# Mixture-of-experts after windowed attention: an earlier second routing phase, four weight fetches on the first queue, and a small gather ahead

## The chip, the core and the metric

The kernel runs on one core of one Trainium2 chip. The metric is the device time of one execution in microseconds; the time before is 681.13 us, the median of three runs. A core has a matmul engine (PE), two elementwise engines (VectorE, DVE here, and ScalarE, ACT here), GpSimd (POOL), and SyncE (SP), which issues DMAs. Each engine takes its instructions in program order; an instruction that waits for another engine holds everything queued behind it on its own engine.

## The reference

Attention over a window of 64 keys gives 4608 rows of 512 values. A gate of 512x8 scores every row for eight experts. The (row, expert) pairs are taken in the order of falling score: a row goes to the expert if it has no expert yet and the expert has fewer than 576 rows. Each expert then runs a two-layer network on its rows.

```python
logits = x @ w_gate
order = np.argsort(-logits.flatten())
for idx in order:
    tok, e = (int(idx) // E, int(idx) % E)
    if assigned[tok] >= 0 or counts[e] >= cap:
        continue
    assigned[tok] = e
    counts[e] += 1
for e in range(E):
    mask = assigned == e
    h = np.maximum(x[mask] @ w1[e], 0.0)
    out[mask] = h @ w2[e]
```

## The kernel before

**Stages.** Attention (to about 160 us) leaves the rows in DRAM as `xs` and the scores in SBUF as `L`. Routing runs in eight phases p = 0 to 7; each finds the expert that fills up next, writes its number to `ei`, and lists its 576 rows in `idx`. Then that expert's rows are gathered, transposed and multiplied, while the routing of later phases goes on between the products. Phase 0 has nothing to run beside; from phase 1 on, routing instructions stand between matmuls of the experts.

**A routing phase** (`Routing.steps`). Phase 1 begins with six operations that find each row's best open expert (`choices`, L446 to L453). Then come eight rounds of a search for the threshold score. In phase 1 a round is: VectorE compares all scores with 15 thresholds (`G`, L461, two instructions), PE counts with nine small matmuls (L532, `rps`), VectorE folds the counts down to `pr` (L538 to L564), PE spreads the result over all partitions (L567), and VectorE picks the next thresholds (L572 to L590). After the rounds come positions (L643, L644), the list (L681, L690) and `idx` (L695). A phase's tail (L702 to L725, one matmul L720 in it) takes the filled expert out of `L`; the next phase needs that.

**An expert.** `turn` gathers the rows with five indirect DMAs issued by POOL (`xg`, L849), PE transposes each (L862, `tp`), ACT takes the high part of the transposed rows (`xh`, L839) and VectorE the rest (`xl`, L843). `load` fetches eight weight chunks of 512 KB into six stage buffers `st` (L780, from SP; for p = 0 from POOL from the fourth chunk on, behind the gathers on POOL). ACT makes each chunk's high part `wh` (L797). The low part `wl` is a VectorE subtraction for the first three chunks of the first expert (L801); for all others ACT writes the negated high part (L806) and POOL issues a DMA that adds the stage buffer to it (L808). `steps` runs 16 units of the first layer (L908: twelve matmuls each, as wh with xh, wl with xh, wh with xl; the unit waits in a PSUM buffer `h`, of which there are three, for ACT's `hh`, L880, and VectorE's `hl`, L885), then the second layer (L940 for the last 64 rows, L950 for the rest).

**What sets the order.** Nothing is scheduled on the chip. `Streams` runs the generators `route`, `load`, `turn` and `steps` against a modelled clock while the program is built: a generator that yields a number is resumed that many nanoseconds later, one that yields a function when it turns true. The order of these resumptions is the order of instructions on every engine. `slack` (from `SLACK[p]`, 0 for the first phase and 100 for the others) is added to the modelled time at several places of every round. Phase 1 is held by `yield lambda: ex.turned` in `route` until the first expert's rows are all transposed. The first expert's chunk 3 is held by the same condition in `load`, and its chunks 3 to 7 follow at 3500 modelled nanoseconds each.

Of the kernel before, what the change touches and what calls it, by code (L numbers as in the profile page):

```python
# [25 lines left out]
DM = H * D  # L26
# [314 lines left out]
NR = 8  # L341
FAR = 2.0 ** 101
OWN = 2
SLACK = (0,) + (100,) * 7
U32 = mybir.dt.uint32


class Routing:


    def __init__(self, ctx, tc, c, V):
        self.tc, self.nc, self.c, self.V = tc, tc.nc, c, V
        nc = tc.nc
        rt = ctx.enter_context(tc.tile_pool(name="rt", bufs=1))
        self.rt, self.ctx = rt, ctx

        def t(name, shape, dt=FT):
            x = rt.tile(shape, dt, name=name)
            setattr(self, name, x)
            return x  # L360

        for name in ("eid", "un", "m", "best"):
            t(name, [128, NJ])
        for name in ("oh", "w", "one"):
            t(name, [128, NJ, E], BF)
        t("G0", [128, NJ, ND], BF)
        t("cw", [128, E])
        t("dg", [128, ND], I32)
        t("lane", [128, 1])
        self.setup = self.constants(c["jp"], t)  # L370
        self.idx, self.eint = {}, {}

    def counters(self):
        iota = self.nc.gpsimd.iota
        iota(self.cw, pattern=[[-1, E]], base=E, channel_multiplier=0, allow_small_or_imprecise_dtypes=True)
        iota(self.dg, pattern=[[1, ND]], base=1, channel_multiplier=0)
        iota(self.lane, pattern=[[0, 1]], base=0, channel_multiplier=1, allow_small_or_imprecise_dtypes=True)

    def constants(self, jp, t):
# [103 lines left out]
    def steps(self, p):  # L483
# [7 lines left out]
        if p < E - 1:  # L491
# [6 lines left out]
            if own:  # L498
                one4 = tile_([128, NJ // 4, 4, 4 * E], BF, name="one4")
                one1 = one.rearrange("p (q k) e -> p q (k e)", k=4)  # L500
                for j0, j1 in ((0, 3), (3, 6), (6, 9)):
                    nc.scalar.copy(one4[:, j0:j1], one1[:, j0:j1, None, :].to_broadcast([128, 3, 4, 4 * E]))
                yield 2000
            M = 128 if own else 32
            q8 = self.all8
            thr = self.tab[:, 0]
            base = tile_([128, 1], I32, name="base")
            rest = []
            for r in range(NR):
                G = tile_([128, NJ, ND], BF, name="G") if p or r else self.G0  # L510

                if not p:
# [183 lines left out]
        self.idx[p] = idx  # L696
        yield self.dve(200)
        if p < E - 1:
            if p == 0:
                yield 3000  # L700
            if not p:
                nc.vector.scalar_tensor_tensor(self.eid, m, T[:, 0:1], best, op0=OP.is_gt, op1=OP.mult)  # L702
            eq = tile_([128, NJ], FT, name="eq")
# [31 lines left out]
NCH = 4  # L735
# [11 lines left out]
class Experts:  # L747
# [17 lines left out]
    def room(self):  # L765
        return self.ps.tile([128, 320], FT, name="h", bufs=3)

    def load(self, p, ei):

        nc, fw = self.nc, self.fw  # L770
# [5 lines left out]
        def fetch(i):  # L776
            st[i] = fw.tile([128, 1024], FT, name="st", bufs=STAGE)

            q, r = (nc.gpsimd, eg) if p == 0 and i >= 3 else (nc.sync, e)
            q.dma_start(st[i], self.part(i, r))  # L780

            there[i] = max(self.clock(), there.get(i - 1, 0)) + \
                (LOAD if p else 1500 if i < 3 else 4000) * (1 if i else 2)

        for i in range(3):
            fetch(i)
        if p == 0:
            yield lambda: self.gathered
        for i in range(2 * NCH):
            if p == 0 and i == 3:  # L790
                yield lambda: self.turned
            yield lambda: self.taken - self.ring < self.used
            if there[i] > self.clock():
                yield there[i] - self.clock()
# [14 lines left out]
                self.spawn(self.ready(p, i, hi, lo), self.busy(650, "pool") + ADDED - 1200)  # L809
                dt = 1300  # L810
            self.taken += 1
            if i + 3 < 2 * NCH:
                fetch(i + 3)
            yield max(100, dt - 1200) if p or i < 3 else 3500

    def ready(self, p, i, hi, lo):
        self.W[p, i] = (hi, lo)
# [175 lines left out]
def body(tc, q, k, v, vt, wg, w1, w2, xs, out):  # L993
    nc = tc.nc
    with ExitStack() as ctx:
# [12 lines left out]

        st = Streams()
        ex.spawn, ex.busy, rt.busy, ex.clock = st.add, st.busy, st.busy, lambda: st.now  # L1010
        ex.warm = rt.warm

        def route():
            for p in range(E):
                if p == 1:
                    yield lambda: ex.turned
                for dt in rt.steps(p):
                    if p in rt.eint and p not in known:
                        known.add(p)
# [32 lines left out]
```

## Time and profile before

| | us |
|---|---|
| median of 3 runs | 681.13 (680.34 to 681.78) |
| the profiled execution | 680.94 |
| its span, first to last instruction | 679.3 |
| PE busy in the span | 640.0 (94%) |
| VectorE, ScalarE, GpSimd busy | 444.7, 362.6, 184.2 |

The profiled execution's own time is 1.6 us over its span and 0.2 us under the median. A row of the timeline gives start, length, engine, line, operation, result and inputs, and in brackets the engine's idle time before it and what ended that. PE is busy 94% of the span, so what matters is where it is not, and where its granted clock is at the lower of its two levels (1.2 and 2.4 GHz; PEclk 1.00 is the upper one).

### The profile page before, as it was taken

The numbers are of one execution on the slowest core, as the hardware profiler recorded it, in microseconds if no ns is written. First come the engines' busy times: TensorE is split into PE (matmuls) and PEld (weight loads), VectorE is DVE, ScalarE is ACT, GpSimd is POOL, SyncE is SP. The second block draws the span as 40 slices with busy tenths as digits, with TensorE's granted clock in tenths as the row PEclk, the third lists the DMA queues.
The fourth block names the chain that finished last, engine by engine and source line by source line (L and its number), as shares of the span: only waits on it lengthen the run. The fifth ranks groups of instructions, "written<-read, shape, count | busy, mean of one in ns | idle before, by whom it ended". The sixth has DMA issues, their size and how long they took to land. (4 is left out here: it accounts for less than half of the span.)

```text
span 679.3 us, 16951 instructions
## 1 busy us (share of the span) xinstructions
PE 640.0 (94%) x6383; PEld 537.4 (79%) x6383; DVE 444.7 (65%) x2246; ACT 362.6 (53%) x733; POOL 184.2 (27%) x217
## 2 busy tenths in 40 slices
PE   7999999997489899799999999999999999999995
PEld 5667777775369678797898799789789879988984
DVE  5888898888767657586687688589668861220300
ACT  4788989884045328325743662753446455634410
POOL 0433133330042116204320630512233064312111
PEclk7999999998589999899999999999999999999999
DMA  9999998912066439907973983987696599972501
GB/s 299 346 368 370 368 325 318 350 65 80 16 235 136 90 120 276 240 2 254 239 145 110 261 199 69 299 196 140 229 226 148 159 247 288 239 203 77 95 24 46
DMA packets 50065, 134.08 MB, mean 197 GB/s; under 512 B 4672, under 2 KB 10944, under 8 KB 49984
## 3 DMA queue, kind: packets, MB, share of 16 engines
q0 software_dynamic: 15392, 53.49, 34.7%
q1 hardware_dynamic: 34048, 79.00, 33.0%
q8 instruction: 50, 0.82, 0.5%
q10 hardware_dynamic: 544, 0.52, 0.2%
q14 instruction: 31, 0.25, 0.1%
HBM read 82.13 MB, written 18.87 MB: 149 GB/s over the span
## 5 line engine op out<-in xcount | busy, mean ns | idle before, releaser
L930 POOL DMA_INDIRECT out<-ot,idx x40 | 41.2, 1029 | 262.1 <-DVE ot L928 48.1
L885 DVE SCALAR_TENSOR_TENSOR hl<-h,hh 128x256 fp32r<-128x256 f32 x128 | 53.4, 417 | 84.7 <-ACT hh L880 84.1
L880 ACT ACTIVATE hh<-h 128x256 fp32r<-128x256 f32 (+1 forms) x128 | 52.4, 409 | 101.5 <-PE h L908 100.2
L950 PE MATMUL o<-wh,hh 128*128 128x512 f32 x256 | 102.6, 401 | 0.0
L950 PE MATMUL o<-wh,hl 128*128 128x512 f32 x256 | 102.2, 399 | 0.0
L950 PE MATMUL o<-wl,hh 128*128 128x512 f32 x256 | 101.4, 396 | 0.0
L908 PE MATMUL h<-xh,wh 128*128 128x256 f32 (+1 forms) x512 | 92.9, 301 | 1.3 <-ACT xh L839 1.3
L135 DVE CUSTOM_DVE_ANT_0 st<-Sp,mask 128x128 f32<-128x128 f32 x288 | 78.7, 277 | 21.8 <-PE Sp L126 14.1
L908 PE MATMUL h<-xh,wl 128*128 128x256 f32 (+1 forms) x512 | 92.9, 300 | 0.0
L145 ACT ACTIVATE pe<-st,mx 128x128 f32<-128x128 f32 x288 | 91.2, 390 | 2.8 <-DVE mx L135 2.8
L908 PE MATMUL h<-xl,wh 128*128 128x256 f32 (+1 forms) x512 | 92.3, 299 | 0.1
L908 PEld LDWEIGHTS h<-xh,wh 128*128 128x128 f32 x512 | 76.1, 191 | 2.1 <-ACT xh L839 1.6
L908 PEld LDWEIGHTS h<-xh,wl 128*128 128x128 f32 x512 | 76.6, 191 | 0.1
L908 PEld LDWEIGHTS h<-xl,wh 128*128 128x128 f32 x512 | 76.2, 191 | 0.4 <-DVE xl L843 0.3
L797 ACT ACTIVATE wh<-st 128x1024 fp32r<-128x1024 f32 x64 | 67.2, 1051 | 10.7 <-DMA st<-w 10.6
L808 POOL DMA_DIRECT2D wl<-st x61 | 56.4, 1176 | 58.8 <-ACT wl L806 50.7
L922 ACT ACTIVATE ot<-o 128x512 f32<-128x512 f32 x32 | 19.1, 598 | 86.4 <-PE o L950 82.9
L806 ACT ACTIVATE wl<-wh 128x1024 fp32r<-128x1024 f32 x61 | 64.5, 1057 | 0.7
L849 POOL DMA_INDIRECT xg<-xs,idx x40 | 40.0, 1000 | 63.2 <-DMA st<-w 40.3
L950 PEld LDWEIGHTS o<-wh,hl 128*128 128x128 f32 x256 | 48.3, 189 | 9.8 <-issue 0.7
L950 PEld LDWEIGHTS o<-wh,hh 128*128 128x128 f32 x256 | 48.4, 189 | 8.8
L950 PEld LDWEIGHTS o<-wl,hh 128*128 128x128 f32 x256 | 48.3, 189 | 8.8
(175 smaller groups left out, 1135.7 us busy)
## 6 DMA issues: line engine op xcount, KB each, us to landing
wl<-st POOLq DMA_DIRECT2D x61, 512.0 KB, 8.1
st<-w SPq DMA_DIRECT2D x59, 512.0 KB, 7.7
xs<-x SPq DMA_DIRECT2D x36, 256.0 KB, 5.3
VO<-v SPq DMA_DIRECT2D x6, 1168.0 KB, 17.1
VT<-vt SPq DMA_DIRECT2D x6, 1152.0 KB, 11.7
Q<-q SPq DMA_DIRECT2D x6, 1152.0 KB, 14.1
K<-k SPq DMA_DIRECT2D x6, 1152.0 KB, 15.6
st<-w POOLq DMA_DIRECT2D x5, 512.0 KB, 6.2
```

The costliest lines, as they stand in the source:

```text
L135: nc.vector.tensor_tensor_reduce(st[:, h, :], Sp[h % 2][:, h // 2], mk, scale=-0.125, scalar=3.0e38, op0=OP.add, op1=OP.min, accum_out=mx[ ...
L145: nc.scalar.activation(pe[:, h, :], st[:, h, :], AF.Exp, bias=mx[:, h:h + 1], scale=-1.0)
L797: nc.scalar.activation(hi, st[i], AF.Copy)
L806: nc.scalar.activation(lo, hi.bitcast(FT), AF.Copy, scale=-1.0)
L808: nc.gpsimd.dma_start(lo.bitcast(FT), st[i], accum_op=OP.add)
L849: nc.gpsimd.indirect_dma_start(out=g[0:n, a], out_offset=None, in_=self.xs, in_offset=IndirectOffsetOnAxis(ap=idx[0:n, a:a + 1], axis=0))
L880: nc.scalar.activation(hh[:, f, c0:c1], h, AF.Relu)
L885: nc.vector.scalar_tensor_tensor(t, h[:, a - c0:b - c0], 0.0, hh[:, f, a:b].bitcast(FT), op0=OP.max, op1=OP.subtract)
L908: nc.tensor.matmul(h, wv[:, cc, 128 * (f % 2):128 * (f % 2) + 128], xt[:, cc, c0:c1], start=(k == 0), stop=(k == 11))
L922: nc.scalar.activation(ot, o, AF.Copy)
L930: nc.gpsimd.indirect_dma_start(out=self.out, out_offset=IndirectOffsetOnAxis(ap=idx[0:m, a:a + 1], axis=0), in_=ot[0:m], in_offset=None)
L950: nc.tensor.matmul(o, ht[:, f, 128 * a:128 * a + 128], wt[:, 512 * (f % 2):512 * (f % 2) + 512], start=(k == 0), stop=(k == 23))
```

## The change

- `SLACK` becomes 0 for phase 1 too, and `route` no longer holds phase 1 back; the 3000 ns pause in the tail of phase 0 goes.
- The phases from `OWN` = 2 on pause 3500 ns instead of 2000 ns after ACT's copies.
- The first expert's fourth chunk is fetched from SP with the first three, and its later chunks from POOL one step further ahead. Chunk 3 waits for two evacuated row tiles instead of all five, and chunks 3 to 7 follow at 900 modelled ns instead of 3500.
- `prime`, in round 4 of phase 0, is one more indirect DMA on POOL: it gathers eight rows of `xs`, by a constant list of row numbers, into a tile that nothing reads.

```diff
-SLACK = (0,) + (100,) * 7
+SLACK = (0, 0) + (100,) * 6
...
+        t("rows", [128, 1], U32)
...
+        iota(self.rows, pattern=[[0, 1]], base=0, channel_multiplier=1)
...
                     nc.scalar.copy(one4[:, j0:j1], one1[:, j0:j1, None, :].to_broadcast([128, 3, 4, 4 * E]))
-                yield 2000
+                yield 3500
...
             for r in range(NR):
+                if not p and r == 4:
+                    self.prime()
...
         if p < E - 1:
-            if p == 0:
-                yield 3000
...
+    def prime(self):
+
+        x = self.fw.tile([8, DM], FT, name="first")
+        self.nc.gpsimd.indirect_dma_start(out=x, out_offset=None, in_=self.xs,
+                                          in_offset=IndirectOffsetOnAxis(ap=self.rows[0:8, 0:1], axis=0))
+
...
-            q, r = (nc.gpsimd, eg) if p == 0 and i >= 3 else (nc.sync, e)
+            q, r = (nc.gpsimd, eg) if p == 0 and i >= 4 else (nc.sync, e)
...
-                (LOAD if p else 1500 if i < 3 else 4000) * (1 if i else 2)
-
-        for i in range(3):
+                (LOAD if p else 1500) * (1 if i else 2)
+
+        ahead = 3 if p else 4
+        for i in range(ahead):
             fetch(i)
...
             if p == 0 and i == 3:
-                yield lambda: self.turned
+                yield lambda: self.tiles[0] > 1
...
-            if i + 3 < 2 * NCH:
-                fetch(i + 3)
-            yield max(100, dt - 1200) if p or i < 3 else 3500
+            if i + ahead < 2 * NCH:
+                fetch(i + ahead)
+            yield max(100, dt - 1200) if p or i < 3 else 900
...
-        ex.warm = rt.warm
+        ex.warm, ex.rows, rt.prime = rt.warm, rt.rows, ex.prime
...
             for p in range(E):
-                if p == 1:
-                    yield lambda: ex.turned
                 for dt in rt.steps(p):
```

The numbers reorder every engine. On VectorE, from the third weight subtraction (`wl<-st,wh`; the first two stand further ahead) to the second low part of the transposed rows (`xl`; its row says x2, the second and the third), this stood before (`c` is the input of the tail's matmul, `rps` its result):

```order
L801 TENSOR_TENSOR wl<-st,wh 128x1024
L709 TENSOR_SCALAR e_4204<-cw,code 128x8
L710 TENSOR_TENSOR L<-L,e_4204 128x288
L713 SCALAR_TENSOR_TENSOR oh<-m,base,one 128x288
L717 TENSOR_REDUCE c_4221<-oh 128x8
L843 TENSOR_TENSOR xl<-tp,xh 128x4x128
L722 TENSOR_TENSOR st<-st,rps 128x8
L724 TENSOR_SCALAR e_4240<-cw,code 128x8
L725 TENSOR_TENSOR st<-st,e_4240 128x8
L843 TENSOR_TENSOR xl<-tp,xh 128x4x128 x2
```

and now this, with line numbers of the changed kernel:

```order
L715 SCALAR_TENSOR_TENSOR oh<-m,base,one 128x288
L719 TENSOR_REDUCE c_4205<-oh 128x8
L810 TENSOR_TENSOR wl<-st,wh 128x1024
L724 TENSOR_TENSOR st<-st,rps 128x8
L726 TENSOR_SCALAR e_4216<-cw,code 128x8
L727 TENSOR_TENSOR st<-st,e_4216 128x8
L810 TENSOR_TENSOR wl<-st,wh 128x1024
L448 TENSOR_REDUCE m<-L 128x36
L852 TENSOR_TENSOR xl<-tp,xh 128x4x128
L449 TENSOR_TENSOR oh<-L,m 128x288
L450 SCALAR_TENSOR_TENSOR w<-oh,cw_331 128x288
L852 TENSOR_TENSOR xl<-tp,xh 128x4x128
```

All of the tail, the last two subtractions and the first three operations of phase 1 (L448 to L450) now stand ahead of the second `xl`; before, phase 1 began after all five.

On ACT, from the first transposed rows on, weight conversions and evacuations stood like this before:

```order
L839 ACTIVATE xh<-tp 128x4x128 x3
L880 ACTIVATE hh<-h 128x256
L839 ACTIVATE xh<-tp 128x4x128
L880 ACTIVATE hh<-h 128x256
L839 ACTIVATE xh<-tp 128x4x64
L880 ACTIVATE hh<-h 128x256
L797 ACTIVATE wh<-st 128x1024
```

and now:

```order
L848 ACTIVATE xh<-tp 128x4x128 x2
L806 ACTIVATE wh<-st 128x1024
L815 ACTIVATE wl<-wh 128x1024
L848 ACTIVATE xh<-tp 128x4x128
L889 ACTIVATE hh<-h 128x256
L848 ACTIVATE xh<-tp 128x4x128
L806 ACTIVATE wh<-st 128x1024
L889 ACTIVATE hh<-h 128x256
L848 ACTIVATE xh<-tp 128x4x64
L815 ACTIVATE wl<-wh 128x1024
```

The conversions of chunks 3 and 4 (`wh`, then `wl`) moved in among the row tiles; the evacuation of the second unit (`hh`) now stands behind the conversion of chunk 4.

On PE, just ahead of the first count of phase 1 (L532), this stood before; six whole units and half of a seventh came first (a row with x4 is four matmuls, a unit has twelve):

```order
L908 MATMUL h<-xh,wh 128x256 x4
L908 MATMUL h<-xh,wl 128x256 x4
L908 MATMUL h<-xl,wh 128x256 x4
L908 MATMUL h<-xh,wh 128x320 x4
L908 MATMUL h<-xh,wl 128x320 x2
L532 LDWEIGHTS one
L532 MATMUL rps<-G,one 32x60
```

and now (the count is L536 in the changed kernel):

```order
L871 MATMUL tp<-identr,xg 128x64 x4
L917 MATMUL h<-xh,wh 128x256 x4
L917 MATMUL h<-xh,wl 128x256 x4
L917 MATMUL h<-xl,wh 128x256 x4
L536 LDWEIGHTS one
L536 MATMUL rps<-G,one 32x60
```

Only three whole units stand ahead of the count now, and the last row tile's transposes (L871) come just before the third.

## Rows read from the trace of the kernel before

**Rows 1.** Two stretches: length, busy time (instructions) by engine, PEclk, DMA share, GB/s.
```profile
275.70:284.90 9.20, 5.39 (x35) 5.12 (x34) 4.39 (x19) 5.37 (x8) 1.74 (x2) 0.81 1.06 249
350.00:668.00 318.00, 317.42 (x2177) 280.85 (x2177) 178.86 (x700) 150.07 (x235) 90.13 (x94) 1.00 0.67 175
```

**Rows 2.** Waits of PE, 198 to 290 us: total, times, longest.
```profile
PE rps L532 <- DVE G L461: 4.1, 2, 3.8
PE h L908 <- ACT xh L839: 1.3, 2, 0.7
```

**Rows 3.** Timeline: the first list of rows, and gathers on POOL.
```profile
189.06 0.17 DVE L695 CAST idx<-h 128x5 uint32<-128x5 f32 x1 [0.35 <-PE h L690]
190.18 2.04 POOL L849 DMA_INDIRECT xg<-xs,idx  x1 [40.30 <-DMA st<-w]
193.81 1.30 POOL L849 DMA_INDIRECT xg<-xs,idx  x1 [0.30 <-issue]
255.50 1.01 POOL L849 DMA_INDIRECT xg<-xs,idx  x1 [1.74 <-DVE eq L704]
```

**Rows 4.** DMA issues at 190 and at 197.5 us: size, us to landing.
```profile
xg<-xs,idx POOLq DMA_INDIRECT x1, 5.6
st<-w POOLq DMA_DIRECT2D x1, 512.0 KB, 5.7
```

**Rows 5.** VectorE by line, 189.2 to 199.5 us: busy us, mean ns, idle before.
```profile
L801 DVE TENSOR_TENSOR wl<-st,wh 128x1024 fp32r<-128x1024 f32 x3 | 3.6, 1222 | 0.8 <-ACT wh L797 0.8
L843 DVE TENSOR_TENSOR xl<-tp,xh 128x512 fp32r<-128x512 f32 x2 | 1.4, 688 | 1.0 <-ACT xh L839 1.0
L717 DVE TENSOR_REDUCE c<-oh 128x8 bf16<-128x288 bf16 x1 | 0.7, 657 | 0.0
...
L722 DVE TENSOR_TENSOR st<-st,rps 128x8 f32<-128x8 f32 x1 | 0.2, 161 | 1.1 <-PE rps L720 1.1
```

**Rows 6.** Timeline: first unit of the first expert, and one operation of `choices`.
```profile
198.09 0.62 PE L908 MATMUL h<-xh,wh 128*128 128x256 f32 x3 [0.69 <-ACT xh L839]
...
199.94 0.74 PE L908 MATMUL h<-xl,wh 128*128 128x256 f32 x4
...
205.80 0.46 DVE L447 TENSOR_TENSOR oh<-L,m 128x288 bf16<-128x288 f32 x1
```

**Rows 7.** Timeline: one run of L940 in the first expert, one in the second.
```profile
229.05 0.40 PE L940 MATMUL o<-wh,hh 128*128 128x512 f32 x1
...
237.58 0.63 PE L940 MATMUL o<-wl,hh 128*128 128x512 f32 x1
...
239.90 0.49 PE L950 MATMUL o<-wh,hh 128*128 128x512 f32 x1
...
301.49 0.39 PE L940 MATMUL o<-wh,hh 128*128 128x512 f32 x1
...
304.91 0.39 PE L940 MATMUL o<-wl,hh 128*128 128x512 f32 x1
```

**Rows 8.** Timeline: the long stop of PE in the second expert.
```profile
276.56 1.06 ACT L797 ACTIVATE wh<-st 128x1024 fp32r<-128x1024 f32 x1 [4.75 <-DMA st<-w]
...
279.69 0.59 PE L532 MATMUL rps<-G,one 128*128 128x60 bf16 x9 [3.81 <-DVE G L461]
```

**Rows 9.** Timeline: the second expert's number, and its first adding DMA.
```profile
247.25 0.14 DVE L730 TENSOR_SCALAR ei<-code 1x1 int32<-1x1 f32 x1
...
261.77 1.97 POOL L808 DMA_DIRECT2D wl<-st  x2
```

**Rows 10.** Timeline: evacuation work on VectorE, and a round in which PE had no product.
```profile
219.87 0.43 DVE L885 SCALAR_TENSOR_TENSOR hl<-h,hh 128x256 fp32r<-128x256 f32 x1
...
233.51 0.41 PE L532 MATMUL rps<-G,one 128*32 128x60 bf16 x9 [0.31 <-DVE q L599]
...
235.86 0.79 DVE L461 TENSOR_TENSOR G<-m,thr 128x300 bf16<-128x300 f32 x2
```

## The prediction

> **What bounds the kernel now.** I read the busy time by stretches first. From 350 to 668 us PE is busy 317.4 of 318.0 us at the upper clock level [rows 1]: there the end is set by the sum of PE's work, which the change leaves alone. So a gain can only come from a place ahead of 350 us where PE stands still or runs at the lower level, and it then carries through to the end unchanged. The waits of PE between 198 and 290 us [rows 2] and the timeline around them show four such places, and the reader is to see in each who came last.
>
> First, the start of expert 0. Its list of rows is ready at 189.06 + 0.17 = 189.23 us, but the first gather is issued at 190.18 and takes 2.04 us, where the same instruction takes 1.01 us at 255.50 [rows 3]; its rows land 5.6 us after issue [rows 4]. The first unit begins at 198.09, its low-part matmuls at 199.94 [rows 6].
>
> Second, the second layer of expert 0. Sixteen L940 matmuls start between 229.05 and 237.58 us; in expert 1 the same sixteen need 301.49 to 304.91 [rows 7]. The weights are late: the first expert's last chunks are converted 3500 modelled nanoseconds apart, and PE waits for their adding DMA.
>
> Third, the start of expert 1: PE waits for `xh` twice, 1.3 us together with 0.7 the longer [rows 2], the shorter 0.6 at this place (the longer is that of the first unit at 198.09, [rows 6]).
>
> Fourth and largest, 275.7 to 284.9 us. ACT waits 4.75 us for a stage buffer of expert 1, holding the evacuation queued behind it; VectorE waits for that evacuation, the thresholds of phase 2 wait on VectorE, and PE stands 3.81 us in front of the count [rows 8], most of the 4.1 us that it waits for thresholds in all [rows 2]. After that the clock is down: 0.81 in the mean of this stretch [rows 1].
>
> **The change part by part.**
>
> Start of expert 0 (A). The small gather runs in round 4 of phase 0, when POOL has nothing to do before the list. If what the first gather pays extra is a first use, the small one pays it: 2.04 − 1.01 = 1.03 us of issue [rows 3] and up to 0.7 of the 0.95 us between list and issue, 1.7 us at best. But PE then meets VectorE. In the new order VectorE does, between the list and the second `xl`, the tail of phase 0 (eleven operations from 0.66 down to 0.16 us, 3.3 us in sum, [rows 5] shows the longest and the shortest), three subtractions of 1.22 us, two `xl` of 0.69 [rows 5], and three operations of `choices` of about 0.46 [rows 6]: 3.3 + 3.7 + 1.4 + 1.4 = 9.8 us, from 189.2 to 199.0. The low-part matmuls of the first unit need that `xl`, so they start at about 199.1 plus a PE wait instead of 199.94. Of this 0.8 us I take off one row tile's transposes, which before lay ahead of that point and now lie behind it (0.5 us): **A gains 0.3 us**. Its ends: 1.7 if VectorE is ahead of my sum, −1.0 if the two clocked waits of PE let the clock sink.
>
> Second layer of expert 0 (B). With chunks 900 ns apart in the plan, and chunk 7's conversion now right after the seventh unit, all adding DMAs land some ten microseconds before L940 wants them. The sixteen starts span 8.53 us against 3.42 in expert 1 [rows 7]: 5.1 more, of which three counts and two spreads of phase 1 that stand in between are work (0.41 us busy for a count [rows 10]; about 0.5 and 0.3 with PE's change between them, an estimate, 2.1 together). That leaves 3.0. The next four matmuls take 2.32 us (237.58 to 239.90) with one count, where 4 × 0.23 + 0.5 = 1.4 would do at the upper level (0.23 is 3.42/15): 0.9 of slow clock. **B gains 3.9 us** (3 to 5).
>
> Start of expert 1 (D) and the long stop (C). The second expert's number is known at 247.25 [rows 9], and everything of that expert follows it: fetches, list, gathers, and the adding DMAs, which POOL issues behind the gathers, the first at 261.77 [rows 9]. In the new order phase 1 starts after three units instead of six and a half. Counted in product time, its list moves up by 4.3 us, that is from 9.0 to 13.3 us ahead of the end of expert 0 (51 us of products). So the adding DMAs, the stage buffers they free, and the fetch ACT waited for at 276.56 come 4.3 us sooner against the products. ACT's wait was 4.75 us, and PE stood only for the 3.81 us at its end because three `h` buffers kept it fed for the time before. With 4.3 of 4.75 gone, the rest is under that cover: **C gains the whole 3.8 us and the slow clock after it**, 0.19 of 9.2 us = 1.7 [rows 1], **5.5 together**. If the cover fails for half, 2.8. All five transposes of expert 1 now also stand well ahead of its first unit: **D gains 0.6 us**. Late next is then nothing on PE up to 350 us that the trace shows.
>
> New waits (E). This is the price. ACT now converts chunk 4 ahead of the second unit's evacuation. Chunk 4 is the first fetch that POOL issues behind the five gathers. Such a fetch went out at 197.5 us [rows 4]; with the first gather cheaper and earlier it goes at about 196.3, and with the landing of 5.7 us [rows 4] it is there at 202.0. ACT converts for 1.06 us [rows 8], to 203.1, evacuates unit 2 and the last row tile (0.4 each), converts again, and only then evacuates unit 3, at about 205.3. VectorE's first fold has that evacuation's `hl` in its middle, so the spread of round 1 can go at 206.6, where PE would be at it at 205.75: 0.85 us of waiting. If the small gather saves nothing, the fetch is 1.3 us later, and so is this. In the other rounds the slack is gone. A round with PE free of products takes from the count at 233.51 to the end of the thresholds at 235.86 + 0.79 = 236.65, 3.1 us [rows 10]; evacuations add 0.43 for `hl` and 0.21 for the last columns per unit on VectorE [rows 10], for some two units a round. The new order gives a round 3.4 to 4.1 us of products plus its own 0.8 on PE. So 3.1 + 1.3 = 4.4 stands against 4.2 to 4.9: most rounds fit, a few wait 0.1 to 0.4. **E costs 1.4 us**, 0.85 + 0.55. Its ends: 0.3 (no evacuation in the way), and 4 (0.85 + 1.3, and 0.25 in every round).
>
> At no cost: one more `iota` at the start, on an idle POOL; 3500 instead of 2000 for later phases, whose lists still come at least 15 us of products ahead of the expert's end, where 9.0 has been enough.
>
> On the gathers themselves a rule could speak against the change. The rows first: the third gather, at 193.81 beside a subtraction on VectorE, took 1.30 us and not 1.01 [rows 3]. The Trainium skill, "SBUF — State Buffer" (the warning on DVE blocking DMA), says that a DMA issued from POOL waits for its descriptors while VectorE runs in a two-port mode, for the whole instruction; by it, five gathers could lose up to a subtraction each. The rows give 0.3 for one of five; the forecast stands on them.
>
> For the small gather a page has another price than the rows. The Trainium skill, "GPSIMD Engine Reference" (Instruction dispatch), puts the first call of freshly loaded code at some 6 us; by it A would be nearer 5 us before VectorE binds. The trace shows 1.03 us more for the first gather, and the sum goes by that.
>
> **Sum.** 0.3 + 3.9 + 5.5 + 0.6 − 1.4 = 8.9 us. Against the profiled execution (680.94 us, 1.6 over its span) that is 672.0 us, a span of 670.4. The median of the runs shown is 681.13, 0.2 away, so the number stands for it too.
>
> **The rivals.**
>
> *ACT starves PE.* The new wait on chunk 4 holds the evacuations longer than the three `h` buffers cover. For it: PE needs buffer 2 again at unit 5, 204 us, and by the working above it is free at 203.9, with no margin. Against it: two of POOL's fetches went to SP or forward, so the DMA queues are emptier. Price 2 to 3 us at full clock: 674.5.
>
> *The long stop stays.* Expert 1's adding DMAs still queue behind its gathers on POOL, and the DMA share is 1.06 through that stretch [rows 1]; if the transfers themselves are the limit, starting 4.3 us earlier brings less. Then C is lost: 677.5.
>
> *VectorE holds the gathers.* VectorE works without a pause beside the five gathers now, and each is slowed as the third was: 0.3 us for each of five [rows 3], 1.5 us on the fetch of chunk 4 behind them: 673.5. Against it: the other gathers in the trace ran beside VectorE's work too and were not slowed. The warning in the Trainium skill, "SBUF — State Buffer", is this mechanism.
>
> *Slower than before.* Without slack PE runs into a wait at each of the sixteen steps of phase 1 (count and spread, eight rounds), and each wait stops the products, in order. It decides at 8.9 / 16 = 0.56 us a step beyond E. For it: the margin I find per round is −0.2 to 0.5 us, and a wait of PE was followed by the lower clock level at 275.7 [rows 1]; half a microsecond at each step with the clock down for ten of the 35 us would cost 8 + 5: 685. Against it: PE's own waiting relaxes the next step, so the margin heals itself.
>
> *The small gather does nothing*, since the extra is no first use: A falls to −0.1 and E grows by 1.3: 673.7.
>
> **How the numbers follow.** Forecast (with its own small deviations) 0.52; ACT starves PE 0.14; the long stop stays 0.09; VectorE holds the gathers 0.05; the small gather does nothing 0.10; slower 0.07; and 0.03 for a loss in some later phase by the new order that cancels the gain. About 0.2% (1.4 us) is what a measurement can tell from no change. The forecast with its ends goes from 667.5 (A 1.7, B 5, E 0.3: 13.1 us) to 677.0 (C 2.8, E 4: 3.6 us); with the starving and the gather cases inside, this leaves the stop that stays in full, the slower case and the cancelled gain outside, 0.19. Faster 0.89, same 0.03, slower 0.08.
>
> **What would show it.** The sixteen L940 starts span under 5 us with no wait for `wl`; between 260 and 285 us no PE wait over 1 us and PEclk 1.00; the low part of the first unit at 199 to 200 us; the first gather near 1.0 us; PE waits for `pr` and `G` between 203 and 240 us of about 1.4 us in sum. I am wrong if those waits come to several microseconds, if ACT's wait for `st` reappears in expert 1, or if PE after 290 us is no longer full.

## The result, and the profile after

The changed kernel takes 672.08 us, median of four runs (670.59 to 673.85); the kernel before took 681.45 beside it. The ratio is 0.9862, interval 0.9828 to 0.9896. The profiled execution is the slowest of the four: 673.85 us, span 672.2, where [rows 1] come from one with a span of 679.3.

First PE by stretches. Columns as in [rows 1]: stretch, its length, busy time of PE, PEld, DVE, ACT, POOL, then PEclk, DMA share, GB/s. The kernel before:

```profile
205.00:228.00 23.00, 23.00 (x186) 21.32 (x185) 17.40 (x70) 12.54 (x20) 4.67 (x6) 1.00 0.56 120
228.00:240.00 12.00, 9.37 (x58) 6.42 (x56) 6.97 (x30) 3.04 (x4) 1.03 (x2) 0.86 0.43 82
240.00:285.00 45.00, 40.58 (x265) 34.14 (x266) 26.71 (x104) 24.52 (x35) 17.28 (x18) 0.96 0.84 223
570.00:600.00 30.00, 30.00 (x215) 28.61 (x213) 10.69 (x29) 23.20 (x35) 8.20 (x9) 1.00 1.00 247
```

and the changed kernel:

```profile
205.00:228.00 23.00, 20.69 (x155) 18.75 (x154) 16.99 (x72) 11.21 (x19) 3.49 (x4) 0.93 0.65 141
228.00:240.00 12.00, 12.00 (x86) 9.73 (x85) 8.02 (x36) 1.91 (x5) 0.00 (x0) 1.00 0.01 2
240.00:285.00 45.00, 44.77 (x321) 38.71 (x320) 32.54 (x130) 26.71 (x40) 17.65 (x18) 1.00 0.85 228
570.00:600.00 30.00, 28.20 (x178) 25.07 (x177) 8.45 (x22) 15.22 (x25) 8.25 (x10) 1.00 1.03 249
```

From 228 to 285 us PE now never stands for long, at the upper clock: the long stop of [rows 8] and the ragged second layer of expert 0 are gone. Two losses are new: 2.3 us and a lower clock ahead of 228, and 1.8 us at 570 to 600, where PE was full before. The waits of PE from 198 to 290 us answer to [rows 2]:

```profile
PE rps L571 <- DVE pr L568: 2.3, 1, 2.3
...
PE rps L536 <- DVE G L463: 0.2, 1, 0.2
```

The timeline of the changed kernel, in the order of the prediction's parts: the five gathers of the list, with the fetches behind them and the three VectorE subtractions beside them [rows 3, 5]; the first unit [rows 6]; the fifth chunk and the first spread; the sixteen L949 [rows 7]; ACT's first long wait in expert 1 [rows 8].

```profile
189.65 0.99 POOL L858 DMA_INDIRECT xg<-xs,idx  x1 [19.77 <-DVE eq L706]
190.94 1.82 POOL L858 DMA_INDIRECT xg<-xs,idx  x1 [0.30 <-issue]
193.07 1.98 POOL L858 DMA_INDIRECT xg<-xs,idx  x1 [0.30 <-issue]
195.35 1.25 POOL L858 DMA_INDIRECT xg<-xs,idx  x1 [0.30 <-issue]
196.91 1.00 POOL L858 DMA_INDIRECT xg<-xs,idx  x1 [0.30 <-issue]
197.90 1.72 POOL L788 DMA_DIRECT2D st<-w  x3
...
190.71 1.23 DVE L810 TENSOR_TENSOR wl<-st,wh 128x1024 fp32r<-128x1024 f32 x1
193.00 1.22 DVE L810 TENSOR_TENSOR wl<-st,wh 128x1024 fp32r<-128x1024 f32 x1
194.56 1.22 DVE L810 TENSOR_TENSOR wl<-st,wh 128x1024 fp32r<-128x1024 f32 x1
...
196.49 0.75 PE L917 MATMUL h<-xh,wh 128*128 128x256 f32 x4 [0.69 <-ACT xh L848]
198.25 0.39 PE L917 MATMUL h<-xl,wh 128*128 128x256 f32 x1 [0.55 <-DVE xl L852]
...
203.61 1.06 ACT L806 ACTIVATE wh<-st 128x1024 fp32r<-128x1024 f32 x1 [2.62 <-DMA st<-w]
207.49 0.17 PE L571 MATMUL rps<-pr,ones 15*128 15x8 bf16 x1 [2.31 <-DVE pr L568]
...
233.28 0.40 PE L949 MATMUL o<-wh,hh 128*128 128x512 f32 x1
237.62 0.39 PE L949 MATMUL o<-wl,hh 128*128 128x512 f32 x1
...
274.11 1.06 ACT L806 ACTIVATE wh<-st 128x1024 fp32r<-128x1024 f32 x1 [0.57 <-DMA st<-w]
```

The first gather is short, but the next three are long, and the fetches go out at 197.90, no earlier than in the kernel before (197.5, [rows 4]). The sixteen L949 start within 4.3 us where it was 8.5. ACT waits 0.57 us where it waited 4.75.

The loss at the step from expert 6 to expert 7, same kernel: a scatter of output rows stands on POOL ahead of the gathers of expert 7, four adding DMAs behind them; ACT waits for a stage buffer, and the transposes wait for ACT and VectorE:

```profile
561.46 1.02 POOL L939 DMA_INDIRECT out<-ot,idx  x1 [9.56 <-DVE hl L894]
562.79 1.00 POOL L858 DMA_INDIRECT xg<-xs,idx  x1 [0.30 <-issue]
...
570.11 3.74 POOL L817 DMA_DIRECT2D wl<-st  x4
...
584.53 1.06 ACT L806 ACTIVATE wh<-st 128x1024 fp32r<-128x1024 f32 x1 [4.65 <-DMA st<-w]
589.04 0.54 PE L871 MATMUL tp<-identr,xg 128*128 128x128 f32 x4 [1.34 <-DVE xl L852]
```

**Marks.** To compare profiles I take the time from the first list (`idx` ready, 189.23 us before, 189.36 after) to the first L940/L949 of an expert. To that of expert 1 it was 112.26 us before and is 103.99: 8.3 gained. To that of expert 6 it was 404.33 and is 394.90: 9.4. To that of expert 7 it was 457.52 and is 450.36: 7.2, which is what reaches the end (span 7.1 shorter).

### The profile page after: what moved, and what is told of

Its sections match the earlier page's. It is cut to its first block, busy times and chain, and to the rows that moved or that the text cites. A ratio compares the mean times of both kernels' runs of the same rounds, so it can differ in the third digit from the quotient of the medians.

```text
span 672.2 us, 16948 instructions
## 1 busy us (share of the span) xinstructions
PE 638.2 (95%) x6383; PEld 536.3 (80%) x6383; DVE 444.0 (66%) x2246; ACT 361.6 (54%) x733; POOL 186.4 (28%) x218
## 5 line engine op out<-in xcount | busy, mean ns | idle before, releaser
L806 ACT ACTIVATE wh<-st 128x1024 fp32r<-128x1024 f32 x64 | 67.2, 1050 | 12.5 <-DMA st<-w 12.4
```

Source lines behind the costliest of these rows:

```text
L806: nc.scalar.activation(hi, st[i], AF.Copy)
```

## The experiments

Three groups of four kernels, each on one chip beside the kernel before. The kernel before itself takes 681.22 to 682.87 us in them, so between groups the ratios to it are compared beside the medians.

| kernel | median (lowest to highest), us | ratio to before | interval |
|---|---|---|---|
| *first group, before 681.22* | | | |
| changed kernel again | 672.64 (672.37 to 674.64) | 0.9879 | 0.9860 to 0.9898 |
| without the small gather | 672.18 (671.58 to 673.05) | 0.9860 | 0.9841 to 0.9880 |
| late subtractions, rounds shifted | 684.11 (682.81 to 685.07) | 1.0036 | 1.0020 to 1.0052 |
| the same, fifth chunk from SP | 684.70 (684.20 to 685.59) | 1.0049 | 1.0032 to 1.0065 |
| *second group, before 682.87* | | | |
| two subtractions alone moved | 672.60 (671.34 to 673.10) | 0.9836 | 0.9814 to 0.9858 |
| routing part alone | 674.04 (673.15 to 674.83) | 0.9864 | 0.9843 to 0.9886 |
| load part alone | 687.68 (686.28 to 688.79) | 1.0063 | 1.0043 to 1.0084 |
| pause back at 2000 | 670.71 (670.02 to 671.98) | 0.9813 | 0.9790 to 0.9836 |
| *third group, before 682.01* | | | |
| changed kernel again | 673.03 (672.41 to 673.31) | 0.9870 | 0.9850 to 0.9890 |
| pause at 2000, all subtractions late | 670.77 (668.64 to 671.49) | 0.9829 | 0.9809 to 0.9849 |
| fifth chunk from SP | 671.41 (670.39 to 672.44) | 0.9843 | 0.9824 to 0.9862 |
| slack of 100 in phase 1 | 713.41 (709.01 to 716.30) | 1.0461 | 1.0430 to 1.0493 |

### The changed kernel again, twice

> The changed kernel once more, unaltered, as the common measure for the other runs on this chip. In its first profiled execution a stop of about 2 us stood at the step from expert 6 to expert 7 (ACT waited 4.65 us for a stage buffer, PE then 1.34 us for xl), and that execution was the slowest of four (673.85 against 670.59 to 672.98). If that stop depends on how DMA transfers happen to fall, it is smaller or absent here in one of the executions and the median is about 672 with a spread of 2 to 3 us. If it is fixed by the order of instructions, the profile shows it again with the same 4 to 5 us on ACT and the first L949 of the last expert again about 2 us later against the one before it than in the kernel before.

> The changed kernel unaltered, beside the three others of this group on the same chip. 0.986 to 0.988 of the kernel before, as in both earlier measurements; the first L949 of expert 7 again 55.5 us behind that of expert 6. If the shorter pause alone made the 670.7 us of the run before, this kernel is 1.5 to 2.5 us over that.

The loss at expert 7 stands in all three profiles, so it is fixed by the order: from expert 6 to expert 7 it took 55.46 us in the first profile, 55.54 and 55.63 in these, 53.19 in the kernel before. ACT waited 4.67 us at that place. The stop at the first spread does vary: 2.31 us in the first profile, 0.49 and 0.6 here, with ACT waiting 0.80 and 0.86 us for the fifth chunk instead of 2.62. It is longest where the first unit came earliest: 7.13 us behind the list in the first profile, 8.09 and 8.47 in these. The spread itself stands 18.13, 17.22 and 17.63 us behind the list: what an early first unit gains, PE waits for there. To the second layer of expert 1 the two take 101.36 and 101.98 us.

### What makes a gather long

Without the small gather:

```diff
-                if not p and r == 4:
-                    self.prime()
```

> The changed kernel without the small gather in phase 0. Theory of the prediction (the first gather's extra microsecond is a first use): the first gather of the list goes back to about 2.0 us with a late issue, everything behind it on POOL moves 1 to 1.7 us later, and the time rises by 1 to 2 us to about 673.5. Rival (a gather is long when a VectorE subtraction of 1.22 us runs beside it, and the first of a program costs nothing extra): the first gather stays at about 1.0 us, the second to fourth stay at 1.3 to 2.0, and the time stays within 0.7 us of the changed kernel.

Two of its gathers on POOL, and the subtraction beside the latter:

```profile
190.20 1.13 POOL L856 DMA_INDIRECT xg<-xs,idx  x1 [40.33 <-DVE e L709]
...
192.97 1.96 POOL L856 DMA_INDIRECT xg<-xs,idx  x1 [0.30 <-issue]
...
192.88 1.22 DVE L808 TENSOR_TENSOR wl<-st,wh 128x1024 fp32r<-128x1024 f32 x1
```

The first gather of the program takes 1.13 us, not 2.0: of the 1.03 us that the prediction gave to a first use, 0.14 are one (0.99 with the small gather). The others take 1.03, 1.96, 1.85 and 0.99. In the kernel before, two subtractions run one behind the other from 0.19 us ahead of its first gather (190.18, 2.04 us, [rows 3]):

```profile
189.99 2.38 DVE L801 TENSOR_TENSOR wl<-st,wh 128x1024 fp32r<-128x1024 f32 x2 [0.76 <-ACT wh L797]
```

The rest of what the small gather saves is in front of that gather: the list to the first gather is 0.96 us without it, 0.29 with it (189.65 − 189.36). The time doesn't move: 672.18 against 672.64.

Then the subtractions, in two ways. The first attempt also changed the modelled time of VectorE, and with it the order of the rounds:

```diff
-                nc.vector.tensor_tensor(lo, st[i], hi.bitcast(FT), OP.subtract)
-                self.W[p, i] = (hi, lo)
-                dt = self.busy(1130, "dve")
+                self.spawn(self.low(p, i, hi, lo, st[i]), 0)
+                dt = 1300
...
+    def low(self, p, i, hi, lo, st):
+        yield lambda: not i or self.lows[0] > i
+        self.busy(1130, "dve")
+        self.nc.vector.tensor_tensor(lo, st, hi.bitcast(FT), OP.subtract)
+        self.W[p, i] = (hi, lo)
+        yield 0
```

> The changed kernel with one thing moved: the subtractions that make the low parts of the first expert's second and third weight chunks stand behind low parts of the row tiles on VectorE instead of beside the gathers. If a subtraction beside it is what makes a gather long, gathers two to four shrink from 1.82, 1.98, 1.25 to about 1.0 us each, POOL issues the fetches behind them about 2 us earlier (at about 196 instead of 197.90), ACT's 2.62 us wait for chunk 4 and PE's 2.31 us wait at the first spread shrink by as much, and the time falls by 1 to 3 us unless the first unit now waits for the moved low parts. If gathers are long for another reason (their own queue, their DRAM rows, the list), they keep their lengths and the time stays or rises.

The third and the fourth gather became short (1.00, 1.82, 0.95, 0.95, 0.93); the second still begins beside the first subtraction, which this edit leaves in place. The time rose by 11.5 us instead of falling. The second list came 11.55 us ahead of the first unit of expert 1 instead of 16.2, and the stop of the kernel before was back: ACT waits 4.56 us for a stage buffer in expert 1.

The second of this pair adds the fetch below and has the same fault:

> The same move of the two subtractions, and the first expert's fifth chunk fetched from SP with the four others instead of from POOL behind the gathers. If PE's 2.31 us at the first spread and the low clock after it come from the late fifth chunk in front of the evacuations on ACT, both waits are gone whatever the gathers do, the first unit starts no later than in the changed kernel, and the time falls by 2 to 4 us to 668 to 670. If the extra 512 KB on the way delay the gathered rows, the first unit starts 0.5 to 1.5 us later and the gain is under 1 us.

It takes 684.70 us and not 668 to 670, though PE no longer waits at the first spread. Neither tells what the subtractions are worth. The second attempt leaves the modelled time as it was (`dt = self.busy(1130, "dve")` stays, `low` has no `busy`), so that two subtractions are all that moves:

> The changed kernel with two VectorE subtractions alone moved (low parts of the first expert's second and third weight chunks, from beside the gathers to behind the second and the third low part of the row tiles); every other instruction stands where it stood, unlike in the run before with the same idea, where the rounds of phase 1 shifted too. Theory: a gather that begins while a subtraction runs ends 0.82 us after the subtraction does. Then gathers three and four take 0.95 to 1.0 us, the fetches behind them go out about 1.5 us sooner (196.3 instead of 197.9), ACT's wait for the fifth chunk shrinks by as much, the stop at the first spread with it, and the time falls by 0 to 1.5 us, less if the first units wait for the moved low parts. Rival for the first late-low run (684 us because the subtractions moved, and not because the rounds shifted): this kernel too takes about 684 us.

```profile
192.95 0.96 POOL L863 DMA_INDIRECT xg<-xs,idx  x1 [0.30 <-issue]
196.39 1.72 POOL L788 DMA_DIRECT2D st<-w  x3
...
197.88 0.74 PE L922 MATMUL h<-xh,wh 128*128 128x256 f32 x4 [1.72 <-ACT xh L853]
...
195.00:205.00 10.00, 8.28 (x60) 7.84 (x58) 8.65 (x17) 6.81 (x11) 4.27 (x7) 0.83 0.90 268
```

Only the second gather, which still begins beside a subtraction, is long (1.81), the third and the fourth take 0.96; the fetches go out 1.5 us sooner, ACT and the first spread don't wait. But PE waited 1.72 us for `xh` ahead of the first unit, the clock fell to 0.83 in the mean of 195 to 205 us, and the first spread stands 17.89 us behind the list, no earlier than in the changed kernel: the wait moved to the first unit. Why `xh` was later in this profile, the rows don't settle. Nothing is gained up to expert 7, whose second layer begins 449.72 us behind the list (449.06 to 450.36 in the changed kernel). The median is within 0.6 us of the changed kernel's three, but the ratio, 0.9836, is lower than its 0.9862 to 0.9879, and the group has no run of it; a gain of some 2 us is not excluded. The rival, 684 us, is: the loss of the run before came with the shifted rounds.

### The fifth chunk

```diff
-            q, r = (nc.gpsimd, eg) if p == 0 and i >= 4 else (nc.sync, e)
+            q, r = (nc.gpsimd, eg) if p == 0 and i >= 5 else (nc.sync, e)
...
-        ahead = 3 if p else 4
+        ahead = 3 if p else 5
```

> The changed kernel with the first expert's fifth chunk fetched from SP, everything else in its place. ACT's wait for that chunk (2.62 us in the first profile, 0.80 in the second) and PE's wait at the first spread of phase 1 (2.31 and 0.5) are gone if the fetch behind the gathers makes them; the time falls by 0.5 to 2 us. If the early 512 KB delay the gathered rows instead, the first unit starts later by as much and the time stays.

Both waits are gone, PE is full from 205 to 228 us (23.00 of 23.00), the first unit comes no later (8.36 us behind the list, 8.47 in the changed kernel beside it), and the spread stands 16.91 us behind the list (17.22 to 18.13 in the changed kernel). So the late chunk in front of the evacuations makes the stop at the first spread. The time is 1.6 us less, 671.41 against 673.03, though the two intervals overlap.

### One part at a time

Routing part alone, with the fetches, the conversions and the hold of chunk 3 as they were:

```diff
-                if not p and r == 4:
-                    self.prime()
...
-            q, r = (nc.gpsimd, eg) if p == 0 and i >= 4 else (nc.sync, e)
+            q, r = (nc.gpsimd, eg) if p == 0 and i >= 3 else (nc.sync, e)
...
-                yield lambda: self.tiles[0] > 1
+                yield lambda: self.turned
...
-            yield max(100, dt - 1200) if p or i < 3 else 900
+            yield max(100, dt - 1200) if p or i < 3 else 3500
```

> Only the part of the change that lets phase 1 begin early: slack 0, no hold, no pause; the first expert's weights are fetched and converted as in the kernel before, and there is no small gather. By the sum of the prediction the gains of the long stop (5.5) and of the start of expert 1 (0.6) come from this part, the gain of 3.9 in the second layer of expert 0 does not, since the weights stay late, and the loss to new waits is smaller because no conversion of chunk 4 stands ahead of the second evacuation: 675 to 677 us. Rival: the early phase 1 only pays with the early weights, because PE waits for the weights at the second layer whatever the routing does: then the time lost there grows by the rounds that no longer fill it, and the total is 679 to 681.

674.04 us, 8.8 under the kernel before: better than either expectation. In the second layer of expert 0 (its L940 is L947 here) PE waits 1.90 us, for the rounds only:

```profile
234.70 0.41 PE L534 MATMUL rps<-G,one 128*32 128x60 bf16 x9 [0.65 <-DVE q L601]
236.37 0.17 PE L569 MATMUL rps<-pr,ones 15*128 15x8 bf16 x1 [1.25 <-DVE pr L566]
...
228.00:240.00 12.00, 10.10 (x64) 7.73 (x64) 8.62 (x41) 3.31 (x5) 1.42 (x2) 1.00 0.50 95
```

But these waits go back to the weights. With the weights late in the plan, this count and this spread stand on PE with no product between them, as they do in the kernel before (count at 233.51, [rows 10]; spread at 235.18). In the changed kernel and in the load part alone eight products stand between a count and its spread there. The sixteen starts span 7.02 us (230.25 to 237.27).

Load part alone (phase 1 behind the rows again):

```diff
-SLACK = (0, 0) + (100,) * 6
+SLACK = (0,) + (100,) * 7
...
-                yield 3500
+                yield 2000
...
-                if not p and r == 4:
-                    self.prime()
...
+            if p == 0:
+                yield 3000
...
+                if p == 1:
+                    yield lambda: ex.turned
```

> Only the part that fetches and converts the first expert's weights sooner; phase 1 waits for the first expert's rows, with slack and pause as in the kernel before. By the sum: 3.9 us gained in the second layer of expert 0, the long stop of expert 1 with ACT's wait for a stage buffer stays or grows, since products of expert 0 end sooner while the routing does not: 677 to 679 us. Rival: weights that come sooner end expert 0 sooner, and all of that gain is lost again in a longer stop at expert 1, 680 to 682.

687.68 us, 4.8 slower than the kernel before. The second layer is full (12.00 of 12.00 from 228 to 240 us, where the kernel before had 9.37); its sixteen starts span 4.34 us with no wait for `wl`, though the rounds come as late as before. All of that gain and more is lost behind it:

```profile
229.04 0.40 PE L949 MATMUL o<-wh,hh 128*128 128x512 f32 x1
233.38 0.39 PE L949 MATMUL o<-wl,hh 128*128 128x512 f32 x1
...
277.67 1.06 ACT L806 ACTIVATE wh<-st 128x1024 fp32r<-128x1024 f32 x1 [6.61 <-DMA st<-w]
...
279.05 1.43 PE L917 MATMUL h<-xh,wh 128*128 128x320 f32 x4 [3.95 <-ACT xh L848]
...
228.00:240.00 12.00, 12.00 (x76) 8.83 (x75) 7.51 (x33) 1.03 (x2) 0.99 (x1) 1.00 0.05 12
240.00:285.00 45.00, 35.47 (x211) 28.55 (x209) 23.49 (x89) 23.72 (x33) 15.64 (x17) 0.89 0.81 220
```

### Slack

```diff
-SLACK = (0, 0) + (100,) * 6
+SLACK = (0,) + (100,) * 7
```

> The changed kernel with the slack of 100 modelled ns back in the rounds of phase 1. The second list's lead over the first unit of expert 1 was 11.05 us in the kernel before (ACT then waited 4.75 us for a stage buffer), 11.55 with shifted rounds (4.56), 16.2 in the changed kernel (0.4 to 0.6). Theory: the stop depends on that lead alone; slack makes each round longer against the products, the lead falls below 16 us and ACT's wait comes back, about 0.8 to 0.9 us for each microsecond of lead lost, with a PE stop of up to 4 us where it passes what three h buffers cover; 673 to 679 us. The slower case of the prediction (no slack, a wait at each step) would have this kernel faster than the changed one.

The direction was right, the size wrong by more than 30 us. At expert 1 the theory holds: lead 11.06 us, ACT waits 5.88. But the same stop stands in every later expert, where I had expected none: ACT waits 4.05, 3.49, 4.64 and 3.65 us for a stage buffer in experts 2 to 5, and worst at the step to the last one, where six adding DMAs stand behind the gathers:

```profile
603.39 5.53 POOL L817 DMA_DIRECT2D wl<-st  x6
...
619.54 1.06 ACT L806 ACTIVATE wh<-st 128x1024 fp32r<-128x1024 f32 x1 [11.95 <-DMA st<-w]
...
621.38 1.44 PE L917 MATMUL h<-xh,wh 128*128 128x320 f32 x4 [10.18 <-DVE hl L894]
```

The third list leads its first unit by 12.5 us here (316.46 to 328.97) and by 17.7 in the changed kernel (306.37 to 324.06), so a later phase 1 delays the phases after it too. The kernel before and the load part alone have the same slack with the shorter pause, and no such stops: from expert 2 to 5 ACT waits at most 0.89 us for a stage buffer there. That points to the longer pause as what the stops need besides; slack with the shorter pause in the changed kernel was not tried, so it is not shown.

Seven kernels side by side; lead is from the start of the second list's `idx` to the first unit of expert 1:

| kernel | lead, us | ACT's longest wait for `st`, 240 to 285 us | PE busy, 240 to 285 us |
|---|---|---|---|
| routing part alone | 19.06 | 0.75 | 45.00 |
| pause back at 2000 | 16.44 | 0.81 | 45.00 |
| changed kernel | 16.17 | 0.87 | 44.77 |
| late subtractions, rounds shifted | 11.55 | 4.56 | 40.91 |
| slack of 100 | 11.06 | 5.88 | 40.10 |
| kernel before | 11.05 | 4.75 | 40.58 |
| load part alone | 12.57, of which PE stood 2.86 for `xl` | 6.61 | 35.47 |

### The pause

```diff
-                yield 3500
+                yield 2000
```

> The changed kernel with the pause behind ACT's copies in the phases from the third on back at 2000 ns from 3500. The gathers of the last expert then stand ahead of the second group of scattered rows of the expert before it on POOL, as in the kernel before. If the new loss of 2.3 us between experts 6 and 7 comes from these gathers and the adding DMAs behind them being held by that scatter, it is gone, and the time falls by 1.5 to 2.5 us to about 670. If it comes from the earlier phase 1 itself (experts shifted against the routing), it stays and the time stays at 672.

670.71 us. On POOL the gathers of expert 7 now begin at 547.71 us, and ACT's wait at the step to expert 7 is halved:

```profile
547.71 1.04 POOL L858 DMA_INDIRECT xg<-xs,idx  x1 [0.30 <-issue]
...
581.40 1.06 ACT L806 ACTIVATE wh<-st 128x1024 fp32r<-128x1024 f32 x1 [2.35 <-DMA st<-w]
...
583.43 0.39 PE L949 MATMUL o<-wh,hh 128*128 128x512 f32 x1
636.81 0.39 PE L949 MATMUL o<-wh,hh 128*128 128x512 f32 x1
```

From expert 6 to expert 7 it is 53.38 us, close to the 53.19 before the change, so the loss came with the longer pause. The ratio is 0.9813, where the changed kernel has 0.9862 to 0.9879; no run of that stands in this group. Last, this pause together with all three subtractions late (the edit against the kernel with two of them moved):

```diff
-        yield lambda: not i or self.lows[0] > i
+        yield lambda: self.lows[0] > i if i else self.tiles[0] > 0
```

> The changed kernel with the pause at 2000 ns and all three VectorE subtractions moved behind the gathers. Theory: no gather begins beside a subtraction, so all five take 0.93 to 1.0 us and the fetches behind them go out 2.4 us sooner, 6.2 us behind the list instead of 8.6; ACT then doesn't wait for the fifth chunk, PE not at the first spread. If the late fetches had cost time, the kernel is 1 to 2 us faster than with the pause alone, 668.5 to 670. Rival: the gathers are not on the path of anything that sets the end, since what they give the fetches the first unit loses to the moved subtractions: within 0.7 us of 670.7.

```profile
193.04 0.95 POOL L863 DMA_INDIRECT xg<-xs,idx  x1 [0.30 <-issue]
196.49 1.18 POOL L788 DMA_DIRECT2D st<-w  x2
```

All five gathers are short (0.93 to 1.08), and the fetches go 6.4 us behind the list instead of 8.2 with the pause alone. But the first low-part matmul now waits 0.90 us for `xl`, not 0.44, and the first spread stands 17.9 us behind the list, not 17.5. The time is that of the pause alone: 0.1 us apart by the medians, 0.0016 by the ratios (0.9829 and 0.9813), which is within their intervals. So the rival was right. Both kernels with the shorter pause beat the changed one; the second was measured beside it, 670.77 against 673.03, and their ranges don't meet.

## Why the prediction came out as it did

The time was forecast at 672.0 (667.5 to 677.0) and is 672.08. That it is so close is luck in part, by errors that cancel: up to the second layer of expert 1 the sum of 8.9 us compares with 8.3, 10.9 and 10.3 in the three profiles, and an edit that I had put at no cost takes 2.3 to 2.4 back at the end.

- **A, start of expert 0 (0.3 forecast).** 1.7 us in the first profile (first unit 8.86 us behind the list before, 7.13 after), 0.8 and 0.4 in the two others. The size is within its ends, the working is not: of the extra that I gave to a first use, the gap ahead of the gather is one (0.96 to 0.29), and 0.14 us of its length; nearly all of the 1.03 us in its length is VectorE. VectorE itself was ahead of my sum, the first low-part matmul came at 198.25 and not at 199.1. The 6 us that the Trainium skill, "GPSIMD Engine Reference" (Instruction dispatch), gives for freshly loaded code don't show in any run here. The rival "VectorE holds the gathers" had the mechanism and nearly the price on the fetch: it went out 1.6 us after my 196.3. What stood against that rival, that other gathers ran beside VectorE's work and were not slowed, was misread, since the long first gather was one of the slowed. Its price on the time is not shown: shorter gathers alone gained nothing clear. In the time the small gather does nothing either (672.18 us without it).
- **E, new waits (1.4 forecast).** The place was right, behind the conversion of the fifth chunk. In the first profile it cost 2.31 us of waiting instead of 0.85; the fetch was 1.6 later than I had it and its conversion began 5.7 us behind it (197.90 to 203.61), as forecast from [rows 4]. The lower clock behind it came on top (0.93 from 205 to 228 us). In the other two profiles the wait was 0.5 to 0.6. The waits for other rounds came to 0.2, not 0.55: no row of PE's waits up to 290 us shows another. A and E are not separate: with the first spread held by that chunk, an early first unit only lengthens the wait (the largest A and the largest E stand in one profile).
- **B, second layer of expert 0 (3.9 forecast).** The gain came, the sixteen starts within 4.3 us instead of 8.5: from 228 to 240 us 2.6 us of PE's time and some 1.7 of clock, 4.3 in sum. The weights are its reason: the load part alone has it in full, the routing part alone gets down to 7.02 us. Two details of the working were wrong. In the kernel before, two counts stand among the sixteen starts and not three (229.38 and 233.51). And the adding DMA is the smaller part of the direct wait; the rest is the round that late weights leave bare on PE. The waits of PE in the kernel before, 200 to 242 us (total, times, longest), have 1.1 for the weights and 1.5 for rounds:

```profile
PE rps L567 <- DVE pr L564: 1.2, 1, 1.2
PE o L940 <- DMA wl<-st: 1.1, 2, 0.8
PE rps L532 <- DVE q L599: 0.3, 1, 0.3
```

- **C and D (6.1 forecast).** PE gained 44.77 − 40.58 = 4.2 us from 240 to 285 us, and the clock rose from 0.96 to 1.00 over 45 us, 1.8: 6.0. The lead grew by 5.1 us (11.05 to 16.17), forecast 4.3, and ACT's wait went from 4.75 to 0.57. In the table every lead of 16 us and more goes with waits of ACT under 1 us, every lead under 13 with waits over 4.5. The lead does not set the size alone: the load part has the longest wait and not the shortest lead.
- **The sum itself.** B and C are not separate terms, as I had added them. B alone makes the products arrive sooner while the list does not, so the stop grows: 4.8 us slower in place of 3.9 faster. The routing part alone, C and D, is as fast as the whole: 0.9864, where the whole is at 0.9862 to 0.9879. The early weights fill the second layer of expert 0 (12.00 us busy against 10.10) and cost 0.5 to 2.3 us at the first spread; in sum they gain nothing that the times show. The ends of the range were also added up wrongly: the terms of the lower one give 12.5 us and not 13.1, so 668.4 us, those of the upper one 677.3; the result lies inside either way.
- **The step that failed in size** is the line "at no cost" on the pause of 3500. I looked at how long ahead of the expert's end the lists come and not at what the gathers then stand behind on POOL: a scatter that waits for products, at 561.46. It cost the 2.3 to 2.4 us. So one sign of being wrong did come: PE after 290 us is no longer full, 28.20 of 30.00 us from 570 to 600.
- **The slower case** (no slack, a wait at each step) has nothing for it: in the first profile, up to 290 us, PE waits at one spread and one count, and slack in phase 1 costs 40 us instead.

## To carry to other kernels

A list or a number that many transfers follow is worth its lead over the work that uses them: measure that lead, since the stop behind it returns as soon as the lead is spent, also by products that get faster. When an edit moves a step, look at what the step then stands behind on each in-order queue, not only at its time in hand. Gains of two edits at neighbouring stalls can be one gain; each alone shows it.

## What the runs showed of the hardware

A gather that POOL issues while one of VectorE's subtractions runs (`wl<-st,wh`, two inputs in SBUF) ends some 0.82 us after that subtraction, as if it could go on only then: 190.94 + 1.82 is 0.82 after the subtraction's end (190.71 + 1.23); 193.07 + 1.98 is 0.83 after 193.00 + 1.22; 195.35 + 1.25 is 0.82 after 194.56 + 1.22; 192.97 + 1.96 in the kernel without the small gather is 0.83 after 192.88 + 1.22. The kernel before shows it too, in a gather of 1.30 us (193.81, [rows 3], 0.82 after 193.07 + 1.22). A subtraction that begins after the gather doesn't hold it: with the pause at 2000 a gather at 195.75 took 0.96, with a subtraction from 195.88 on. The subtractions keep their 1.22 us. A reduction does not hold a gather: in the kernel before one of 0.66 us began at 195.38, the gather at 195.41 beside it took 0.95. The Trainium skill, "SBUF — State Buffer" (Who interferes with whom), says that VectorE with two inputs in SBUF contends with GpSimd's reads, and that a reduction never does; the rows agree, and the gathers of this kernel behave as such readers.

The warning on DVE blocking DMA, on that page of the Trainium skill, has a DMA issued from POOL wait for VectorE's two-port modes; by it the prediction weighed five gathers at up to a subtraction each. The warning does not name an operation with two inputs in SBUF, yet three of the five were held by one: two for most of a subtraction (1.82 and 1.98 us, where the first took 0.99), one for a quarter of a us (1.25).
